# Long convolution and soft mixture of experts: the steps without the first stage rearranged, additions moved to GpSimd, the last batch's rows loaded in two parts, and a new order for the last pairs

## Chip, cores and metric

The kernel runs on one core of a Trainium2 chip. The metric is the device time of one execution in microseconds, as the median of several runs. All data are fp32.

## The reference, cut to what matters

```python
Xf = np.fft.rfft(x, n=2*S, axis=1)          # x: (8, 5696, 128), h: (5696, 128)
Hf = np.fft.rfft(h, n=2*S, axis=0)
y  = np.fft.irfft(Xf * Hf[None], n=2*S, axis=1)[:, :S, :]
x  = y.reshape(B*S, D)                       # 45568 tokens of 128
logits = x @ phi                             # 32 slots: 8 experts of 4
d = softmax(logits, axis=0)                  # over all tokens
slot_input = d.T @ x
slot_out[e] = relu(slot_input[e] @ w1[e]) @ w2[e]
c = softmax(logits, axis=1)                  # over the slots
return c @ slot_out
```

A causal convolution along the sequence by Fourier transforms comes first. Its result goes through a soft mixture of experts: a softmax over all tokens collects one input for each slot, small two-layer networks work on the slots, and a softmax over the slots hands the results back to the tokens. The first softmax needs the running maximum and sum over every token, so no output can be made before the last token has been seen.

## The kernel before, in words

The transform of length 2 x 5696 is factored into 90 by 64 by matrix products, and the work goes in stages that are pipelined over the steps of one loop (`for t in range(last_front + 1)`, L547). There are 9 images: the filter h and 8 batches.

Stage A (`stage_a`, L204) takes a chunk of an image, multiplies with a table (L211) and stores to the DRAM scratch `f`. It runs for t < NA = 72. Its input is folded on GpSimd (`fold`, L195).

Stage B works on units of which an image has 23, three to a step. `load_g` (L224) loads a unit of `f` on SP's queue, four units ahead. `stage_b1` (L235) is a group of small matmuls into the PSUM tile `bt` (L244), of which there is one buffer, and three VectorE operations: the products `pr` (L265) and `pi` (L268), which read PSUM, and their sum `yf` (L270), which reads two SBUF tiles. `stage_b2` (L274) takes `yf` through a second group of matmuls (L284), ScalarE copies the result (L288), and SP stores it to the DRAM scratch `z` (L289). b2 runs one unit behind b1.

Stage C works on pairs of column blocks, 4 to a batch, 32 in all, one to each two steps. `load_pair` (L309) loads a pair's rows of `z` in two transfers (block 0 of 64 rows, 1024 KB, and block 1 of 26 rows, 416 KB) into a tile `zc`. `stage_c1` (L323) has two halves of eight matmuls (L336); between the halves it calls the function `between`, and it returns a function `after`. The halves are folded on VectorE (L341, L342), and `after` does the second fold and four additions on GpSimd (L355), two of them on VectorE in the tail. `stage_c2` (L360) transposes the four quarters of y (L364); `stage_c3` makes logits (L373) and `lt`; `column_max` updates the running maximum on VectorE (L384 to L392); `stage_c4` (L398) transposes `lt` (L402), takes exponentials and row maxima, fills a part of `dt` on GpSimd (L410) and subtracts on GpSimd (L418); `stage_c5` transposes `dt` (L425); `softmax` (L431) normalises the rows, its last product on GpSimd (L438); `dispatch` (L442) accumulates the slot inputs (L449, L454); `stage_c6` (L469) transposes the combine weights (L473) and keeps them in the DRAM scratch `c_t`, or in the tail in the SBUF tile `cT`. In the tail `load_c` (L487) brings the kept weights back as tiles `cl`, four pairs at a time in two buffers, and `place_all` (L493) copies them into `cT` on GpSimd and ScalarE.

The schedule is manual: every engine runs its instructions in the order in which the program issues them, and each waits for its operands and its buffer. SP's queue has nearly all transfers, in that order too. `slot_b` (L561) puts in one b1 and the b2 of the unit before. In a step with odd t and t >= 72, before the change, the order is: slot, c1 of pair T with c4 of pair T-1 between its halves, slot, load of pair T+1, the fold and additions of `after`, c5, slot, softmax. In a step with even t it is: dispatch, slot, c2, c6, slot, c3, slot, column_max. `last_front` is 80; that step has only two units, and pair 26 in c2 and c3.

In these steps z has one buffer, `zc`. After the loop a second tile `zd` is made in memory that the front has left; 6 rows of zeros are copied into it by a transfer (L643), and then pair 28, the first of the last batch, is loaded (L646). Its matmuls read 96 rows only (`used`). The first-layer weights w1 are loaded in eight transfers of 512 KB, one a step from t = 73 (L631) and the last after the loop (L647). The tail loop (L680) takes V = 27 to 31: c2, dispatch of V-1, c6 of V-2, c3, column_max, placing of kept weights, c1 of a later pair with c4 between, c5, softmax; the second-layer weights w2 are loaded in V = 28 and 29 (L713). V = 31 ends with `join_quarters` (L499), which brings four partial maxima together, and its dispatch.

Then come the slot networks (L723 to L778) with one c6 between (L756), and the output: for each batch, row groups of 4, 4 and 3 are multiplied (L803), copied by ScalarE and VectorE (L812, L810) and stored (L814) through five buffers `o`.

Of the kernel before, what the change touches and what calls it, by code (L numbers as in the profile page):

```python
# [74 lines left out]
def kernel(  # L75
# [159 lines left out]
    def stage_b1(u):  # L235
        g, i = divmod(u, NU)
        n = min(2, NP - 2 * i)
        t_ = gs.pop(u)
        tag = "bz" if g == 0 and i % 2 else "bt"
        bt = bps.tile([P, 2, 512], F32, name="bt", tag=tag)  # L240
        for a in range(2):
            r = slice(a * HP, (a + 1) * HP)
            for q in range(n):
                nc.tensor.matmul(bt[q * HP:(q + 1) * HP, a, 0:2 * D], wt[r, 2 * i + q, :],  # L244
                                 t_[r, q, :, :].rearrange("p c d -> p (c d)"),
                                 start=True, stop=True)
        r = slice(0, n * HP)
        pv = bt[r, :, 0:2 * D].rearrange("p a (c d) -> p a c d", c=2)
        if g == 0:
            for a in range(2):  # L250
                pr = bpool.tile([P, 2, D], F32, name="ph", tag="pi" if a else "pr")
                for c in range(2):
                    nc.scalar.activation(pr[r, c, :], pv[:, a, c, :], AF.Copy,  # L253
                                         scale=turn[r, 0, i, a:a + 1])
                nc.vector.scalar_tensor_tensor(  # L255
                    out=Hr[r, i, a, :], in0=pv[:, a, 1, :], scalar=turn[r, 1, i, a:a + 1],
                    in1=pr[r, 0, :], op0=AL.mult, op1=AL.add)
                nc.vector.scalar_tensor_tensor(
                    out=Hi[r, i, a, 0, :], in0=pv[:, a, 0, :], scalar=turn[r, 1, i, a:a + 1],
                    in1=pr[r, 1, :], op0=AL.mult, op1=AL.subtract, reverse1=True)  # L260
            nc.gpsimd.tensor_scalar(out=Hi[r, i, :, 1, :], in0=Hi[r, i, :, 0, :], scalar1=-1.0,
                                    scalar2=None, op0=AL.mult)
            return
        pr, pi = [bpool.tile([P, 2, 2, D], F32, name=f"p{c}", tag=f"p{c}") for c in "ri"]
        nc.vector.tensor_tensor(out=pr[r, :, :, :], in0=pv,  # L265
                                in1=Hr[r, i, :, :].unsqueeze(2).broadcast_to([n * HP, 2, 2, D]),
                                op=AL.mult)
        nc.vector.tensor_tensor(out=pi[r, :, :, :], in0=pv, in1=Hi[r, i, :, :, :], op=AL.mult)  # L268
        y_ = bpool.tile([P, 2, 2, D], F32, name="yf", tag="yf", bufs=2)
        nc.vector.tensor_tensor(out=y_[r, :, :, :], in0=pr[r, :, :, :], in1=pi[r, :, ::-1, :],  # L270
                                op=AL.add)
        prods[u] = y_
# [23 lines left out]
    zn = used = None  # L296
# [12 lines left out]
    def load_pair(T):  # L309
# [3 lines left out]
        t_ = zring.pop(0)  # L313
        zring.append(t_)
        w_ = 2 * 2 * CH * 2 * D
        for r, n, p in z_blocks(N1):
            nc.sync.dma_start(
                out=t_[p:p + n, :, :, :, :, :].rearrange("k h o n c d -> k (h o n c d)"),
                in_=zd[b].rearrange("q (a r) c d -> (q a) (r c d)",
                                    a=2)[r:r + n, j * w_:(j + 1) * w_])  # L320
        zs[T] = t_

    def stage_c1(T, between):  # L323
        t_ = zs.pop(T)
        kr = used if t_ is zn else P
# [7 lines left out]
        def product(o, tab, q):  # L333
            p = bank()
            for h_ in range(2):
                nc.tensor.matmul(p[h_ * HP:(h_ + 1) * HP, :], i1[0:kr, tab, :],  # L336
                                 t_[0:kr, h_, o, :, q, :], start=True, stop=True)
# [9 lines left out]
        between()  # L347
        b_, a_ = product(1, 1, 0), product(1, 2, 1)
        nc.scalar.activation(om[:, :, :], b_, AF.Copy)

        def after():
# [6 lines left out]
        return after  # L358

    def stage_c2(T):  # L360
        for k in (3, 1, 0, 2) if tail else (3, 2, 1, 0):
# [185 lines left out]
    for t in range(last_front + 1):  # L547
# [22 lines left out]

        for tab, src, first, n, k in ((wt, t_w, LAG_B - 2, NP, 2 * PER),
# [5 lines left out]
        if t < NA:  # L577
            stage_a(t, 0)
            fold(t + 1, 0)
# [4 lines left out]
        if t == last_front:  # L584
            assert T is None and U is None and not us[1:]
            slot_b()
            stage_c2(pair(1))
            slot_b()
            assert not us and not wait_b2
            V = pair(1)  # L590
            stage_c6(V - 2)
            stage_c3(V)
            column_max(V)
            break
        rows = (lambda: None) if U is None else (lambda: stage_c4(U))
        after = None
        if T is not None:
            after = stage_c1(T, rows)
        else:
            rows()  # L600
        if pair(1) is not None:
            stage_c2(pair(1))
# [5 lines left out]
        if t < NA:  # L608
            load_x(t + 3)
# [4 lines left out]
        if t < NA:  # L614
            stage_a(t, 1)
            fold(t + 1, 1)
# [9 lines left out]
        if t == NA:  # L626
            lead.close()
            wts = inner.enter_context(tc.tile_pool(name="wts", bufs=1, side="right"))
            w1s = wts.tile([P, E, F], F32, name="w1s")
        if NA < t <= NA + E:  # L630
            nc.sync.dma_start(out=w1s[:, t - NA - 1, :], in_=moe_w1[t - NA - 1])  # L631

    T = V + 1
    (_, n0, p0), (_, n1, p1) = z_blocks(N1)
    gap, used = slice(p1 + n1, p0), p0 + n0
# [4 lines left out]
    zn = last.tile([P, 2, 2, CH, 2, D], F32, name="zd")  # L642
    nc.sync.dma_start(out=zn[gap, :, :, :, :, :].rearrange("k h o n c d -> k (h o n c d)"),  # L643
                      in_=zring[0][gap, :, :, :, :, :].rearrange("k h o n c d -> k (h o n c d)"))
    zring.insert(0, zn)
    load_pair(V + 2)  # L646
    nc.sync.dma_start(out=w1s[:, E - 1, :], in_=moe_w1[E - 1])  # L647
# [5 lines left out]

    after = stage_c1(T, lambda: stage_c4(V))
    after()
    stage_c5(V)
    softmax(V)
# [22 lines left out]
    for V in range(T, NT):  # L680
        if V > T:
            stage_c2(V)
        dispatch(V - 1)
        stage_c6(V - 2)
        if V == T:
            stage_c2(V)
# [6 lines left out]
        if N < NT:  # L693
            after = stage_c1(N, lambda: stage_c4(V))
            load_pair(N + 2)
        else:
            stage_c4(V)
        if after:
            after()
# [3 lines left out]
        if V == NT - 1:  # L703
            join_quarters()
            dispatch(V)
        softmax(V)
        if V == T:
            ybufs.insert(0, y_)
            stage_c1(T + 2, lambda: None)()
            load_pair(T + 4)  # L710
        else:
# [4 lines left out]
    stage_c6(NT - 2)  # L716
    assert list(Ls) == [NT - 1] and not (ys or ds or prods or gs or zs or xs or folded or wait_b2
# [26 lines left out]
    for g in range(EG):  # L744
        for f0 in range(0, F, FH):
            p = bank()
            for q in range(Q):
                nc.tensor.matmul(p[q * NSL:(q + 1) * NSL, :], siz[:, g * Q + q, :],
                                 w1s[:, g * Q + q, f0:f0 + FH], start=True, stop=True)
# [6 lines left out]
    stage_c6(NT - 1)  # L756
# [34 lines left out]
    assert NV * RW == R1 - 1  # L791
    G4 = 4
    for b in range(B):
        for w0 in range(0, NV, G4):
            n = min(G4, NV - w0)
            lone = b == B - 1 and w0 + G4 >= NV
# [53 lines left out]
```

## Time and profile before

| | us |
|---|---|
| median of 5 runs | 952.52 |
| lowest and highest of them | 948.92, 963.72 |
| the profiled execution | 950.38 |
| span of its profile | 948.6 |
| TensorE busy | 845.9 |
| VectorE busy | 670.4 |
| ScalarE busy | 522.6 |
| GpSimd busy | 446.4 |

The mean clock that TensorE was granted is 0.95 of full speed. The page of the profile has the busy time of each engine, then the span in 40 equal slices with the busy share of each in tenths and the granted clock (PEclk), then the transfers, then the chain of waits that ended last, and then groups of instructions, where PE is TensorE, DVE VectorE, ACT ScalarE, POOL GpSimd and SP SyncE. A line of a group gives the line of the code, the engine, the operation, output and inputs with their shapes, the count, the busy time in us and the mean in ns, and the idle time of the engine ahead of them with what ended it. L numbers are lines of the kernel before.

### The profile page before, as it was taken

To read this page: it belongs to the slowest core of one execution; us is meant where nothing else is said; L and a number is where in the kernel's file an instruction comes from. 1 tells how busy PE (TensorE), PEld (TensorE's weight loads), DVE (VectorE), ACT (ScalarE), POOL (GpSimd) and SP (SyncE) were. 2 spreads that over 40 slices of the span, in tenths; PEclk is the share of its full clock that TensorE was granted. 3 is DMA by queue.
4 is the path that set the end of the run, shared out by engine and by line. 5 is a ranking of instruction groups with operands and counts; after the bars stand their busy time and mean duration, and the time that the engine had idled before them with its cause. 6 is when DMAs were issued, how large, how long until landed. Compare 5 with 4: busy or idle time off the path is not lost.

```text
span 948.6 us, 20396 instructions
## 1 busy us (share of the span) xinstructions
PE 845.9 (89%) x7220; PEld 405.1 (43%) x7220; DVE 670.4 (71%) x1140; ACT 522.6 (55%) x1068; POOL 446.4 (47%) x408
## 2 busy tenths in 40 slices
PE   6867788889999999999999999989998887877893
PEld 2322233334444444444444444434443334345883
DVE  3034577577878878887888788868889996593552
ACT  3557645445666665665666566656664443385442
POOL 4646533235655555555555555545543333482000
PEclk9989999999999999999999999999999997797955
DMA  6998899999999999999999999999988976862698
GB/s 171 273 277 266 263 334 311 308 328 299 313 280 318 313 293 294 315 316 292 309 309 318 283 299 338 295 273 308 309 275 288 310 256 193 254 225 97 251 406 333
DMA packets 174239, 272.51 MB, mean 287 GB/s; under 512 B 14982, under 2 KB 119686, under 8 KB 171253
## 3 DMA queue, kind: packets, MB, share of 16 engines
q1 hardware_dynamic: 173563, 270.86, 89.9%
q8 instruction: 58, 0.95, 0.4%
q10 hardware_dynamic: 576, 0.36, 0.2%
q14 instruction: 42, 0.34, 0.1%
HBM read 142.85 MB, written 128.21 MB: 286 GB/s over the span
## 4 chain that ended last, share of the span: by engine, by line
PE 63%; DMA 21%; DVE 4%; issue 4%; POOL 3%; ACT 2%; SPq 2%; DVEq 0%; ACTq 0%; POOLq 0%
PE bank L211 20%; PE bank L336 12%; PE bt L244 10%; DMA gt<-f 7%; DMA f<-fst 7%; PE bz L284 7%; DMA out_dram<-o 4%; PE bank L364 3%; POOL y L355 2%; PE bank L449 2%; PE bank L402 2%; PE bank L373 2%; PE bank L425 2%; DMA zc<-z 1%; PE bank L473 1%
## 5 line engine op out<-in xcount | busy, mean ns | idle before, releaser
L211 PE MATMUL bank<-x,s 128*128 128x512 f32 x576 | 286.4, 625 | 9.8 <-POOL x L200 8.1
L200 POOL TENSOR_TENSOR x<-xc 128x512 f32<-128x512 f32 x144 | 183.5, 1276 | 145.4 <-PE bank L211 108.3
L213 ACT ACTIVATE fst<-bank 128x512 f32<-128x512 f32 x288 | 168.3, 597 | 93.8 <-PE bank L211 69.7
L288 ACT ACTIVATE zst<-bz 128x512 f32<-128x512 f32 (+1 forms) x184 | 108.3, 588 | 169.8 <-PE bz L284 156.4
L265 DVE TENSOR_TENSOR pr<-bt,Hr 128x512 f32<-128x512 f32 (+1 forms) x184 | 127.0, 690 | 103.0 <-PE bt L244 100.0
L244 PE MATMUL bt<-gt,wt 64*64 64x256 f32 x1620 | 138.0, 403 | 50.0 <-DMA gt<-f 17.2
L270 DVE TENSOR_TENSOR yf<-pr,pi 128x512 f32<-128x512 f32 (+1 forms) x184 | 153.7, 835 | 6.4
L211 PEld LDWEIGHTS bank<-x,s 128*128 128x128 f32 x576 | 100.5, 193 | 133.5 <-issue 88.9
L268 DVE TENSOR_TENSOR pi<-bt,Hi 128x512 f32<-128x512 f32 (+1 forms) x184 | 125.2, 681 | 0.0
L284 PE MATMUL bz<-yf,vt 64*64 64x256 f32 x1440 | 116.7, 383 | 6.0 <-DVE yf L270 3.9
L336 PE MATMUL bank<-zc,i 128*64 128x512 f32 x480 | 119.4, 621 | 0.0
L244 PEld LDWEIGHTS bt<-gt,wt 64*64 64x64 f32 x1620 | 44.4, 132 | 166.7 <-PE bank L211 58.8
L355 POOL TENSOR_TENSOR y<-y,op 128x512 f32<-128x512 f32 x64 | 77.6, 1212 | 71.5 <-DVE op L341 69.0
L355 POOL TENSOR_TENSOR y<-y,om 128x512 f32<-128x512 f32 x54 | 76.4, 1414 | 2.1
L410 POOL MEMSET dt<- 64x8 f32 x32 | 3.4, 107 | 146.4 <-ACT dn L413 80.8
L284 PEld LDWEIGHTS bz<-yf,vt 64*64 64x64 f32 x1440 | 53.7, 133 | 41.9 <-issue 11.6
L255 DVE SCALAR_TENSOR_TENSOR Hr<-bt,turn,ph 128x128 f32<-128x128 f32 (+1 forms) x46 | 16.0, 349 | 75.7 <-ACT ph L253 75.7
L364 PE MATMUL bank<-ident,y 109*128 109x109 f32 x512 | 58.8, 269 | 2.2 <-POOL y L355 1.5
L364 PEld LDWEIGHTS bank<-ident,y 109*128 109x128 f32 x512 | 51.2, 146 | 15.0 <-issue 11.6
L366 ACT ACTIVATE yt<-bank 128x360 f32<-128x360 f32 x128 | 51.8, 472 | 4.8 <-PE bank L364 4.8
L336 PEld LDWEIGHTS bank<-zc,i 128*64 128x64 f32 x480 | 30.0, 139 | 54.6 <-issue 48.4
L803 PE MATMUL op<-so,cT 32*128 32x128 f32 x704 | 46.3, 369 | 4.9 <-ACT o L812 4.4
(97 smaller groups left out, 893.7 us busy)
## 6 DMA issues: line engine op xcount, KB each, us to landing
f<-fst SPq DMA_DIRECT2D x288, 180.0 KB
gt<-f SPq DMA_DIRECT2D x198, 256.0 KB
z<-zst SPq DMA_DIRECT2D x176, 256.0 KB
zc<-z SPq DMA_DIRECT2D x30, 1024.0 KB
xc<-in_x_dram SPq DMA_DIRECT2D x64, 320.0 KB
out_dram<-o SPq DMA_DIRECT2D x16, 1024.0 KB
zc<-z SPq DMA_DIRECT2D x30, 416.0 KB
out_dram<-o SPq DMA_DIRECT2D x8, 768.0 KB
```

Of the source, the lines that this page charges most:

```text
L200: nc.gpsimd.tensor_tensor(out=y_[:, :, :], in0=t_[:, 0, :, :], in1=t_[:, 1, ::-1, :], op=AL.subtract if comp else AL.add)
L211: nc.tensor.matmul(p[:, :], s1[:, tab[G], :], src[:, :, :].rearrange("p n d -> p (n d)"), start=True, stop=True)
L213: nc.scalar.activation(st[:, :, G, :], p[:, :].rearrange("p (n d) -> p n d", d=D), AF.Copy)
L244: nc.tensor.matmul(bt[q * HP:(q + 1) * HP, a, 0:2 * D], wt[r, 2 * i + q, :], t_[r, q, :, :].rearrange("p c d -> p (c d)"), start=True, sto ...
L265: nc.vector.tensor_tensor(out=pr[r, :, :, :], in0=pv, in1=Hr[r, i, :, :].unsqueeze(2).broadcast_to([n * HP, 2, 2, D]), op=AL.mult)
L268: nc.vector.tensor_tensor(out=pi[r, :, :, :], in0=pv, in1=Hi[r, i, :, :, :], op=AL.mult)
L270: nc.vector.tensor_tensor(out=y_[r, :, :, :], in0=pr[r, :, :, :], in1=pi[r, :, ::-1, :], op=AL.add)
L284: nc.tensor.matmul(bz[a * HP:(a + 1) * HP, q, 0:2 * D], vt[r, i, a, :], y_[r, a, :, :].rearrange("p c d -> p (c d)"), start=True, stop=True)
L288: nc.scalar.activation(st[:, 0:n, :], bz[:, 0:n, 0:2 * D], AF.Copy)
L336: nc.tensor.matmul(p[h_ * HP:(h_ + 1) * HP, :], i1[0:kr, tab, :], t_[0:kr, h_, o, :, q, :], start=True, stop=True)
L355: eng.tensor_tensor(out=part_, in0=part(v, 0), in1=o_[:, :, :], op=sign)
L364: nc.tensor.transpose(p[:, i * TR:(i + 1) * TR], ys[T][0:TR, k * CH + i, 0:D], ident[0:TR, 0:TR])
```

## The change

It has these parts.

1. Steps with t >= 72 get a function of their own, `without_a`, and a slot of another form, `slot_around`, that puts b1 of a unit ahead of a part of stage C and b2 of the unit before behind it. `stage_c1` no longer takes `between`; it returns `second`, the second half, which returns `after`. `stage_c2` takes the quarters that it is to do.
2. `stage_b1` takes the engine of the addition `yf`. In these steps four of six go to GpSimd; in the last step (t = 80) the additions of both units stay on VectorE.
3. A second z buffer `zd` is made at t = 72 in the memory that stage A leaves, filled with zeros by GpSimd (128x4096), and put ahead of `zc` in the ring. The copy of zero rows and the 96-row matmuls are gone. The load of pair 28 is split: block 0 is issued at the head of the last step, block 1 after its last z store.
4. w1 becomes two tiles. The first four experts are loaded at t = 73 to 76; the other four in one transfer of 2 MB in the tail, after the load of pair 31.
5. The tail loop ends at V = 30 and takes c2 and c3 of pair 31 in beside c4 of pair 30. c4, c5 and dispatch of pair 31 follow the loop, then the last kept weights are placed. c6 of both last pairs stands between the two layers of the slot networks.
6. In the first batch the output's row groups are 1, 3, 4 and 3.

The diff, cut to its core:

```diff
-    def stage_b1(u):
+    def stage_b1(u, adder=nc.vector):
...
-        nc.vector.tensor_tensor(out=y_[r, :, :, :], in0=pr[r, :, :, :], in1=pi[r, :, ::-1, :],
-                                op=AL.add)
+        adder.tensor_tensor(out=y_[r, :, :, :], in0=pr[r, :, :, :], in1=pi[r, :, ::-1, :],
+                            op=AL.add)
...
-        between()
-        b_, a_ = product(1, 1, 0), product(1, 2, 1)
-        nc.scalar.activation(om[:, :, :], b_, AF.Copy)
+        def second():
+            b_, a_ = product(1, 1, 0), product(1, 2, 1)
+            nc.scalar.activation(om[:, :, :], b_, AF.Copy)
+            return lambda: after(a_)
...
+        def slot_around(part, adder):
+            fresh = bool(us)
+            if fresh:
+                u = us.pop(0)
+                prefetch(u + AHEAD)
+                stage_b1(u, adder)
+                wait_b2.append(u)
+            part()
+            if len(wait_b2) > fresh:
+                stage_b2(wait_b2.pop(0))
+
+        def without_a():
...
+            if T is not None:
+                slot_around(lambda: add(stage_c1, T), nc.gpsimd)
+                def middle():
+                    stage_c4(U)
+                    add(kept_[0])
+                slot_around(middle, nc.gpsimd)
+                load_pair(pair(-2))
+                kept_[1]()
+                slot_around(lambda: stage_c5(U), nc.vector)
+                softmax(U)
+                return
+            if t == last_front:
+                load_pair(V + 2, (0,))
+            slot_around(lambda: dispatch(pair(3)), nc.vector)
+            slot_around(lambda: stage_c2(V, (3, 2)), nc.vector if t == last_front else nc.gpsimd)
+            slot_around(lambda: stage_c2(V, (1, 0)), nc.gpsimd)
+            if t == last_front:
+                load_pair(V + 2, (1,))
+            stage_c6(pair(5))
+            stage_c3(V)
+            column_max(V)
+
+        if t == NA:
+            lead.close()
+            wts = inner.enter_context(tc.tile_pool(name="wts", bufs=1, side="right"))
+            zn = wts.tile([P, 2, 2, CH, 2, D], F32, name="zd")
+            nc.gpsimd.memset(zn[:, :, :, :, :, :], 0.0)
+            zring.insert(0, zn)
+            w1s = [wts.tile([P, E // 2, F], F32, name="w1a")]
+        if NA < t <= NA + E // 2:
+            nc.sync.dma_start(out=w1s[0][:, t - NA - 1, :], in_=moe_w1[t - NA - 1])
...
-    zn = last.tile([P, 2, 2, CH, 2, D], F32, name="zd")
-    nc.sync.dma_start(out=zn[gap, :, :, :, :, :].rearrange("k h o n c d -> k (h o n c d)"),
-                      in_=zring[0][gap, :, :, :, :, :].rearrange("k h o n c d -> k (h o n c d)"))
-    zring.insert(0, zn)
-    load_pair(V + 2)
-    nc.sync.dma_start(out=w1s[:, E - 1, :], in_=moe_w1[E - 1])
+    w1s.append(last.tile([P, E // 2, F], F32, name="w1b"))
...
-    for V in range(T, NT):
+    for V in range(T, NT - 1):
...
         else:
             stage_c4(V)
-        if after:
-            after()
+            stage_c2(V + 1)
+            stage_c3(V + 1)
...
-        if V == NT - 1:
-            join_quarters()
+        if N == NT:
+            column_max(V + 1)
             dispatch(V)
         softmax(V)
         if V == T:
...
             load_pair(T + 4)
+            nc.sync.dma_start(out=w1s[1][:, :, :],
+                              in_=moe_w1[E // 2:].rearrange("e d f -> d e f"))
...
-    stage_c6(NT - 2)
+    stage_c6(NT - 3)
+    stage_c4(NT - 1)
+    stage_c5(NT - 1)
+    join_quarters()
+    dispatch(NT - 1)
+    softmax(NT - 1)
+    while landed:
+        placed_c()
...
-    stage_c6(NT - 1)
+    for T in list(Ls):
+        stage_c6(T)
...
-        for w0 in range(0, NV, G4):
-            n = min(G4, NV - w0)
+        for w0, n in ((0, 1), (1, 3), (4, 4), (8, 3)) if b == 0 else ((0, 4), (4, 4), (8, 3)):
```

## The prediction on record

> **What bounds the kernel now.** I read the page's 40 slices first. A slice is 23.7 us; digits are busy tenths.
> ```profile
> PE   6867788889999999999999999989998887877893
> DVE  3034577577878878887888788868889996593552
> POOL 4646533235655555555555555545543333482000
> PEclk9989999999999999999999999999999997797955
> ```
> TensorE (PE) fills slices 11 to 29. From slice 30 (711 us) on it has gaps, VectorE (DVE) reads 9, and at slice 33 the clock falls. From 711 us the first stage is finished, and this is what the change touches. The windows view, one line per two steps, then the last step (t = 80) with what follows:
> ```profile
> 719.29:738.90 19.61, 16.49 (x184) 7.51 (x187) 18.29 (x31) 9.38 (x19) 7.17 (x7) 1.00 0.91 306
> 738.90:758.52 19.62, 16.49 (x185) 7.51 (x187) 18.37 (x32) 9.39 (x19) 7.32 (x7) 1.00 0.89 298
> 758.52:778.15 19.63, 16.49 (x184) 7.51 (x187) 18.37 (x32) 9.38 (x19) 7.33 (x7) 1.00 0.85 285
> 778.15:797.40 19.25, 14.83 (x132) 7.70 (x134) 12.06 (x21) 6.69 (x13) 7.20 (x6) 0.76 0.55 176
> ```
> Columns after the length: PE, weight loads, VectorE, ScalarE, GpSimd, PE clock, DMA share, GB/s. A double step takes 19.6 us and VectorE is busy 18.3 of it: VectorE bounds it, with TensorE waiting in turn. The chain of waits (start, us, what) of one double step agrees:
> ```profile
> 719.95 0.69 DVE pr L265
> ...
> 721.27 0.69 DVE yf L270
> 721.97 0.61 DVE op L341
> ...
> 722.65 1.20 POOL y L355
> ...
> 723.91 2.78 POOL y L355 x2
> ...
> 726.76 1.21 POOL y L355
> ...
> 728.01 0.59 PE bank L364 x4
> ```
> So c2 also waits for the last of four GpSimd additions. In the tail the same view shows transfers:
> ```profile
> 801.56 9.80 DMA zc<-z
> ...
> 811.55 3.30 PE bank L336 x8
> ...
> 820.09 8.95 DMA zd<-z
> ...
> 843.02 8.49 DMA cl<-c_t
> ```
> c1 of pair 28 starts 3.4 us late, and its eight matmuls take 3.30 us where the same eight take 1.87 at full clock: the wait costs twice.
>
> **What the Trainium skill says.** "TensorE: Matmul & The Clock Gate", What's actually happening: the clock halves after an idle window of about 3.4 us and needs as long a busy one to recover. The trace agrees: after gaps around 784 to 788 us the windows show 0.50 from 789 to 798, and again 813 to 822. "GPSIMD Engine Reference", Performance versus the Vector engine: a two-input fp32 addition is about 2 times slower than on VectorE. The groups by form:
> ```profile
> L270 DVE TENSOR_TENSOR yf<-pr,pi 128x512 f32<-128x512 f32 x18 | 15.0, 833 | 0.6
> L355 POOL TENSOR_TENSOR y<-y,om 128x512 f32<-128x512 f32 x6 | 8.5, 1415 | 0.2
> L355 POOL TENSOR_TENSOR y<-y,op 128x512 f32<-128x512 f32 x6 | 7.1, 1187 | 6.8 <-DVE op L341 6.6
> ```
> Here it is 1.19 us alone and 1.41 beside VectorE. "SBUF — State Buffer", Who interferes with whom: a VectorE operation with two SBUF inputs contends with GpSimd, one with a single SBUF input does not. The trace agrees: yf is 0.69 us alone and 1.11 beside GpSimd; pr and pi (one input in PSUM) stay at 0.68.
>
> **The change, part by part.** I walked the new program order of each engine by hand with the trace's spacings (VectorE: pr, pi 0.6 each, fold 0.7 each, yf 0.7 or 1.05; TensorE: b1 0.6, b2 0.45, c1 half 1.87, c4 and c5 0.6, dispatch 1.02, c2 half 0.83, c6 0.5, c3 0.75).
>
> *1. Double steps.* Four of six yf leave VectorE; the two that stay are those beside L355. 4 x 0.7 = 2.8 us go: 18.3 becomes 15.5. But two new idles come. The next b1 waits for the single bt buffer, and with yf gone nothing fills that gap on VectorE: 0.75. And column_max now follows c3 with no unit between. From the last b1 TensorE does half of c2, b2, c6 and c3 (2.53), ScalarE's lt 0.6 more: 3.15, of which pr and pi fill 1.3; 1.85 idle, with the next pr queued behind. 15.5 + 2.6 = **18.1 us** in place of 19.6. Other bounds are below: TensorE's spacings sum to about 15.0 to 16.5, GpSimd 7.2 + 4 x 1.19..1.41 = 12.0 to 12.8, DMA 306 GB/s x 19.6/18.1 = 331 GB/s (slices reach 338) in the two double steps with w1, lower later since half of w1 moves out. The moved addition in the even step sits behind the four L355 and L438; I get its end 0.4 us ahead of its b2, so no wait. c2 no longer waits on L355. From b1 of unit 184 (714.31) to b1 of unit 205 (783.45) are 69.1 us now; 3 x 18.1 + 9.05 = 63.4 then: **gain 5.7**. Bounds: 2 (each moved addition exposed by 0.5 us) to 10 (TensorE-bound at 16.5, idles filled).
>
> *2. The zero fill of the new z buffer* (128x4096, GpSimd, at t = 72). No such row; the page's fills of 64x8 in 0.108 and 128x128 in 0.205 us give 0.8 ns an element, 3.4 us; VectorE's 128x4096 took 3.47. It queues behind L438, which ends at 710.3, or until 711.4 behind the store of the freed buffers: done at 713.7 to 714.9. The addition of unit 183, moved to GpSimd, queues behind it; then b2(183) on TensorE, and behind that c6, c3 and b1(184). 1.2 + 0.4 + 1.3 on top gives b1(184) at about 717.2 where it is 714.31: **loss 2.9** (0 to 4.5; zero if the first unit's load lands later anyway). TensorE idles 712 to 715; half a chance of half clock for some 1.5 us: **loss 0.8**.
>
> *3. Last step and z in two goes.* t = 80 now runs from b1(205) to the end of c3 in 12.6 us (783.45 to 796.05), much of it at half clock. In my walk TensorE's longest gap is 1.45 us, the clock holds, and it takes 8.3: **gain 4.3**. The last z store leaves 7.6 us after b1(205), where it was 10.8. Block 0 (1 MB) goes at the head of the step into a buffer free since c1 of pair 26. Block 1 (416 KB) waits for the store to land (now 2.8 us from its data at 794.2 to the load's issue at 797.0; I take 2.2, the copy of the gap rows being gone): issue at +9.8. At the 200 to 380 GB/s of those windows it moves in 1.1 to 2.1 us; with some 2 us to land, as for the store, it is there by +13 to +14. c1(28) is ready for it at +19.3. So the 3.4 us wait goes, and what is late next is VectorE. From c3's end to the fold of pair 28's second half are 23.6 us now (796.05 to 819.65). Without the wait (3.4), and with c1 of 27 and 28 and c4 at full clock (3.01, 3.30, 1.11, 3.64 in place of 1.87, 1.87, 0.59, 1.87: 4.9, some of it hidden) my walk has 15.6: **gain 8.0** (2 to 9). The gap copy on SP and the partial rows fall away at no cost: 96x64 and 128x64 matmuls share the 592 ns minimum.
>
> *4. w1's second half* (2 MB, one transfer) is queued on SP behind pair 31's load and ahead of the third cl load. With that load 3.5 MB, some 9 to 10 us at 350 to 400 GB/s, done 3 us ahead of where ScalarE and GpSimd take cl; what is hidden here is hidden by V = 28's VectorE work. **0** (loss up to 3).
>
> *5. New final order.* c2 and c3 of pair 31 move beside c4 of pair 30. ScalarE still stands at the fifth cl copy (DMA, 851.5), so little moves: by my walk c4(31) comes 0.9 us earlier (861.2 for 862.05), c6(30) leaves the path ahead of L723 (0.5), and comes back between hid and hidT (0.5): **gain 0.9** (-1.5 to 4).
>
> *6. Output.* The first store waits now for 32 matmul passes (1.29) and two copies (1.29). With one row group 0.3 + 0.65: it starts 1.7 us earlier, but only 256 KB; the transfers are the bound after that: **gain 1.0** (0 to 1.7).
>
> Sum: 5.7 - 2.9 - 0.8 + 4.3 + 8.0 + 0 + 0.9 + 1.0 = 16.2. The profiled execution took 950.4 (span 948.6 and 1.8 around it): 934.2. The median of the runs is 2.1 above it: **936**.
>
> **The rivals.**
> A: *The transfers take the tail's gain.* For: pair 28's load took 12 us from its issue (799.3 to 811.4) with others behind it, far over what 1.44 MB need, and if the tracking of z is by whole tensor, block 0 is not early. Then block 1 lands at +21.8 where c1 is ready at +19.3: 2.5 us, and with it the half clock (3.7): 6.2, so 942. Against: 416 KB instead of 1.44 MB. Chance 0.2.
> B: *The front gains more.* The fill hides (3.7 back) and column_max's idle is filled by other VectorE work (1 us in 3.5 double steps): 936 - 7.2 = 929. Against: VectorE and TensorE keep program order. Chance 0.2.
> C: *Slower: GpSimd becomes the bound of the double step.* It has one place: the even step's addition behind L418, four L355 and L438. At 1.41 us it ends 0.4 us in time. From about 2.6 us a pass it decides: the chain 7.55 + 4 x 2.8 + 1.05 + 2.8 = 22.6, then b2, c6, c3, lt: a double step of 25 instead of 18.1, x 3.5 = 24: 960. Against it are the rows above: 1.41 at worst. Chance 0.05.
>
> **How the numbers follow.** Forecast 936 with chance 0.55 (its own 932 to 940), A 0.2, B 0.2, C 0.05. The range takes in A and B with some of their spread: 927 to 945. Some 0.5% (5 us) is what a measurement of this kernel tells from no change; A and the forecast are faster, C slower, a doubled A near the same: 0.92, 0.03, 0.05.
>
> **What would show it.** 1: windows of double steps at 18.1 us, VectorE near 15.5, GpSimd near 12.5, VectorE idle ahead of L384 (mx). 2: a GpSimd fill near 711 us and b1(184) at 717. 3: clock 1.00 through 780 to 825, no DMA wait ahead of c1 of pair 28. 5: ScalarE still waiting for cl. 6: first store 2.6 us less 1.7 after the first L803. I am wrong if the double step stays above 19, if half clock persists in the tail, or if c1(28) or c1(29) waits for z.

## The result, and the profile after

The changed kernel takes 947.41 us (median of 37 executions, 938.53 to 959.43); the kernel before takes 956.56 us over its 72 executions. The ratio is 0.9921 with a 95% interval of 0.9902 to 0.9940: faster by 0.8%, or 7.5 us, where 16.2 us were forecast. Ratios leave out executions more than 1.5% above the fastest of their kernel, which is why this one says less than the difference of the medians (9.1 us), and the second profile of the kernel before that is used below (961.99 us; the fastest took 946.82) is of that kind. The time lies outside the range on record (927 to 945). The profiled execution of the changed kernel took 946.73 us (span 944.9), that of the kernel before 950.38.

The page of the changed kernel, the span in 40 slices:

```profile
DVE  3034567577878887888888788888886778773542
POOL 5636632235655554555555555565556565563000
PEclk9979999999999999999999999999999899997966
```

Against the slices before, counted from 1: GpSimd is at 5 and 6 from slice 31 to 35, where it was at 3 and 4, and VectorE, which read 9 in slices 31 to 33, is at 6, 7 and 7. The clock's dip in slices 34 and 35 (7 and 7 before) is gone, there is a new one in slice 32 (8), and the dip at 37 and in the last two slices is still there.

A double step of the changed kernel, from one column_max to the next, in a window with the same columns as before:

```profile
739.49:758.93 19.44, 16.32 (x182) 7.43 (x184) 16.13 (x28) 9.50 (x19) 12.66 (x11) 1.00 0.83 266
```

It is 19.4 us long, as the next one is, 0.2 less than before; VectorE's busy time fell from 18.3 to 16.1, and GpSimd's rose to 12.7 as expected. So VectorE now idles 3.3 us of each.

The gain by stages, from two profiled executions of each kernel (the second pair belongs to the first experiment below). c1(23) means the first matmul of c1 of pair 23, b1(184) that of b1 of unit 184.

| stage | before | after | gain | forecast |
|---|---|---|---|---|
| issue of pair 23's load to c1(23) | 12.1, 12.1 | 17.6, 17.8 | -5.6 | -3.7 |
| c1(23) to c1(27) (double steps, last step) | 81.1, 79.6 | 78.4, 75.9 | +3.2 | +10.0 |
| c1(27) to c1(30) | 33.2, 38.0 | 27.7, 24.4 | +9.5 | +8.0 |
| c1(30) to the first output matmul | 53.6, 56.8 | 56.1, 56.2 | -1.0 | +0.9 |
| first output matmul to the end | 65.8, 65.9 | 64.8, 64.8 | +1.0 | +1.0 |
| sum | 245.7, 252.3 | 244.6, 239.2 | +7.1 | +16.2 |

The sum is near the 7.5 us of the ratio, but it is the mean of 1.1 us in the first pair of executions and 13.1 in the second. The stages show where the 9 us went: 6.8 in the double steps and the step after them, 1.9 in the fill's wait, 1.9 in the stretch with the new final order, with 1.5 more than forecast in the tail to set against them. Stages differ by some us between executions of one kernel (33.2 and 38.0), so single us here are not settled.

### The profile page after: what moved, and what is told of

Read it like the earlier page. It is cut to its first block, busy times and chain, and to the rows that moved or that the text cites. A ratio compares the mean times of both kernels' runs of the same rounds, so it can differ in the third digit from the quotient of the medians.

```text
span 944.9 us, 20432 instructions
## 1 busy us (share of the span) xinstructions
PE 838.5 (89%) x7220; PEld 399.3 (42%) x7220; DVE 661.5 (70%) x1127; ACT 522.5 (55%) x1070; POOL 469.6 (50%) x424
## 4 chain that ended last, share of the span: by engine, by line
PE 67%; DMA 16%; issue 5%; DVE 5%; ACT 2%; POOL 2%; SPq 2%; DVEq 0%; POOLq 0%; ACTq 0%
PE bank L211 22%; PE bt L244 11%; PE bank L336 10%; PE bz L284 8%; DMA gt<-f 5%; DMA out_dram<-o 4%; PE bank L366 4%; DMA f<-fst 3%; PE bank L451 3%; PE bank L375 2%; PE bank L427 2%; PE bank L404 2%; DMA cl<-c_t 1%; SPq L217 1%; PE bank L475 1%
## 5 line engine op out<-in xcount | busy, mean ns | idle before, releaser
L270 DVE TENSOR_TENSOR yf<-pr,pi 128x512 f32<-128x512 f32 (+1 forms) x169 | 145.3, 860 | 5.9
L244 PEld LDWEIGHTS bt<-gt,wt 64*64 64x64 f32 x1620 | 45.2, 133 | 170.5 <-PE bank L211 56.1
L336 PE MATMUL bank<-zc,i 128*64 128x512 f32 x448 | 109.2, 610 | 0.7 <-DMA zc<-z 0.7
L357 POOL TENSOR_TENSOR y<-y,op 128x512 f32<-128x512 f32 x64 | 78.7, 1230 | 60.0 <-DVE op L341 57.4
L357 POOL TENSOR_TENSOR y<-y,om 128x512 f32<-128x512 f32 x54 | 74.4, 1378 | 2.1
L255 DVE SCALAR_TENSOR_TENSOR Hr<-bt,turn,ph 128x128 f32<-128x128 f32 (+1 forms) x46 | 16.1, 349 | 75.8 <-ACT ph L253 75.8
L368 ACT ACTIVATE yt<-bank 128x360 f32<-128x360 f32 x128 | 51.5, 471 | 16.2 <-PE bank L366 16.2
L366 PE MATMUL bank<-ident,y 109*128 109x109 f32 x512 | 56.8, 263 | 1.0 <-DVE y L357 0.7
L366 PEld LDWEIGHTS bank<-ident,y 109*128 109x128 f32 x512 | 49.1, 142 | 14.9 <-issue 13.5
L386 DVE TENSOR_REDUCE mx<-lt 64x1 f32<-64x360 f32 x64 | 33.0, 516 | 29.5 <-ACT lt L378 29.1
L440 POOL TENSOR_TENSOR L<-L,rs 128x512 f32<-128x512 f32 x32 | 44.8, 1399 | 11.3 <-DVE rs L439 5.2
```

Source lines behind the costliest of these rows:

```text
L270: adder.tensor_tensor(out=y_[r, :, :, :], in0=pr[r, :, :, :], in1=pi[r, :, ::-1, :], op=AL.add)
L336: nc.tensor.matmul(p[h_ * HP:(h_ + 1) * HP, :], i1[:, tab, :], t_[:, h_, o, :, q, :], start=True, stop=True)
L357: eng.tensor_tensor(out=part_, in0=part(v, 0), in1=o_[:, :, :], op=sign)
L366: nc.tensor.transpose(p[:, i * TR:(i + 1) * TR], ys[T][0:TR, k * CH + i, 0:D], ident[0:TR, 0:TR])
```

## The experiments

Theory T1, from the two traces: *the double step is a loop of dependent work over several engines and not one engine's busy time; the zero fill delays the front by its place in GpSimd's queue; the second half of w1 and the early block 0 cost or give something in the tail; the new final order gives nothing.* The rivals are, by part: that the idle comes from the single product buffers, that the GpSimd additions give the time, that nothing is gained from where transfers are put. Ratios below are against the kernel before, run on the same chip. Line numbers in a view are those of the kernel that it shows; in the changed kernel c2 is L366 (L364 before), c3 L375 (L373) and its copy lt L378, column_max L386 (L384), c6 L475 (L473), GpSimd's four additions L357 (L355), and the placing of the kept weights L497 (L495).

### Both kernels again

> The kernel before, unedited, for a second profile. Theory 1 (the two profiles differ by chance ahead of 700 us and in the tail's waits): double steps at 19.6 us again, the load of pair 23 issued some us earlier or later than 702.8, and the stretch from it to the end, 245.8 us in the first profile, longer by 2 to 6 us, since the medians differ by more than the profiles. Rival (the first profile is typical): 245.8 within 1 us.

> The changed kernel, unedited, on the same chip as the next ones: ratio 0.992. Theory 1: double steps at 19.4 us again, b1 of unit 184 some 16.6 us after the load of pair 23 (the fill of the second z buffer), a DMA wait of 2 to 4 us ahead of c1 of pair 30; where the clock halves differs. The stretch from pair 23's load to the end 244.6 us, within 3. Rival (one unlucky execution): double steps near 18.1 and no such waits.

The kernel before took 961.99 us in one execution (span 960.2); the changed one has a ratio of 0.9943 [0.9912, 0.9973]. The fill's delay is there again (17.8 us from pair 23's load to c1(23)), and the double steps again take 19.4. In this execution the first double step had no half clock, which the first profile had (21.9 us from column_max to column_max). From pair 23's load to the end the two kernels took 252.3 and 239.2 us, 6.6 more and 5.4 less than in the first profiles and both outside what was expected, so one trace does not tell some 5 us of the whole.

### The fill later

```diff
         if t == NA:
...
-            nc.gpsimd.memset(zn[:, :, :, :, :, :], 0.0)
...
         if t >= NA:
             without_a()
+            if t == NA:
+                nc.gpsimd.memset(zn[:, :, :, :, :, :], 0.0)
```

> The changed kernel with the fill of the second z buffer issued at the end of step 72 instead of its head. Theory 1 (the fill holds the addition of unit 183 on GpSimd, and TensorE behind it): b1 of unit 184 comes 12 to 12.5 us after the load of pair 23 instead of 16.6, TensorE keeps full clock there, and the time falls by 4 to 7 us: ratio to before 0.985 to 0.988. Rival (the first unit's load sets b1(184) in any case): less than 1 us, ratio 0.992.

The front of the changed kernel, GpSimd's timeline and then the chain of waits:

```profile
709.22 3.52 POOL L621 MEMSET zd<- 128x4096 f32 x1 [1.45 <-DMA z<-zst]
```

```profile
714.00 0.65 PE bz L284 x4
714.65 0.92 PE bank L475 x4
715.57 1.36 PE bank L375 x8
716.93 1.06 PE bt L244 x8
```

The fill waits 1.45 us for a store to land (the view names one of z), runs 3.52 us, and the addition of unit 183 stands behind it in GpSimd's order. TensorE waits for that addition until 714.00, comes back at half clock (four matmuls of L475 take 0.92 us, and 0.52 later), and b1 of unit 184 starts at 716.93. Now the same view of GpSimd with the fill behind the step's work:

```profile
710.20 1.25 POOL L270 TENSOR_TENSOR yf<-pr,pi 64x512 f32<-64x512 f32 x1 [2.14 <-DVE pi L268]
711.40 3.51 POOL L634 MEMSET zd<- 128x4096 f32 x1
```

The addition goes first, and the fill lies in a stretch in which GpSimd has nothing else. The ratio is 0.9890 [0.9851, 0.9930] from six executions, beside 0.9943 for the changed kernel on the same chip; c1(23) starts 13.4 us after its load, 4.3 earlier than with the fill ahead. T1 holds here: in the six executions, here and below, with an addition behind the fill c1(23) comes 17.3 to 19.0 us after its load, and in the five of its variants without one 12.8 to 13.4. The ratios differ by 0.5% (some 5 us), which fits, though their intervals overlap; T1 had wanted a little more (0.985 to 0.988).

### All additions on VectorE

```diff
-                slot_around(lambda: add(stage_c1, T), nc.gpsimd)
+                slot_around(lambda: add(stage_c1, T), nc.vector)
...
-                slot_around(middle, nc.gpsimd)
+                slot_around(middle, nc.vector)
...
-            slot_around(lambda: stage_c2(V, (3, 2)), nc.vector if t == last_front else nc.gpsimd)
-            slot_around(lambda: stage_c2(V, (1, 0)), nc.gpsimd)
+            slot_around(lambda: stage_c2(V, (3, 2)), nc.vector)
+            slot_around(lambda: stage_c2(V, (1, 0)), nc.vector)
```

> The changed kernel with all additions yf back on VectorE, the order kept. Theory 1 (a double step is VectorE's path from the column maximum to the fifth unit's product, 15.3 us, and TensorE's from there to the next maximum, 4.1; two of the moved additions lie on that path): the double step becomes 20.6 us instead of 19.4, and the fill no longer holds an addition, so step 72 is 4 us shorter; in all 0 to 2 us slower than the changed kernel, ratio 0.992 to 0.994. Rival (the moved additions come back as contention and waits on GpSimd, so that moving them is worth nothing): the double step stays at 19.4 to 19.6 and the time falls by 4 us, ratio 0.988.

A double step of this kernel:

```profile
761.80:782.60 20.80, 16.25 (x182) 7.39 (x184) 18.99 (x31) 9.51 (x19) 7.25 (x7) 1.00 0.75 236
```

The new order alone makes the double step longer by 1.2 us (20.8 for 19.6). Yet the ratio is 0.9922 [0.9892, 0.9951], no worse than the changed kernel's (0.9943 on the same chip): with no addition on GpSimd nothing stands behind the fill, and c1(23) is 12.8 us after its load. As put in, the four moved additions give 1.4 us a double step, 3.5 times, 4.9 us, and cost 4.9 us behind the fill. That balance is a sum and not settled to the us: in this trace c1(23) to c1(27) takes 84.1 us for 75.9, since the last step too is longer (11.7 us for 9.4), in part at half clock.

### Only the odd step's additions on GpSimd

The last two of the four replacements above, without the first two.

> The changed kernel with the two moved additions of each even step back on VectorE, those of the odd steps still on GpSimd. Theory 1 (the even step's two lie where VectorE waits for TensorE anyway, so moving them gives nothing, and they are what makes step 72 wait for the fill): double step 19.3 to 19.6, c1 of pair 23 at 12.5 to 13.5 us after its load instead of 17.6, 4 to 5 us less: ratio 0.986 to 0.991. Rival (each moved addition is worth its 0.7 us): double step 20.8, which eats the gain: ratio 0.993.

```profile
760.60:780.00 19.40, 16.36 (x183) 7.46 (x184) 17.47 (x29) 9.52 (x20) 10.12 (x9) 1.00 0.83 270
```

The double step stays at 19.4 with VectorE busy for 17.5 of it, and c1(23) is 12.8 us after its load; the ratio is 0.9904 [0.9871, 0.9937]. So the two additions moved in the even step give nothing to the double step, and one of them stands behind the fill at t = 72. All 1.4 us come from the odd step's two.

### The kernel before with the odd step's additions on GpSimd

```diff
-    def stage_b1(u):
+    def stage_b1(u, adder=nc.vector):
...
-        slot_b()
+        moved = nc.gpsimd if t > NA and t % 2 else nc.vector
+        slot_b(moved)
...
-        slot_b()
+        slot_b(moved)
```

> The kernel before with the additions of the first two units of each odd step without the first stage on GpSimd, nothing else. Theory 1 (the old double step of 19.6 us is a loop over GpSimd's four additions of c1, c2's last quarter and TensorE, as its chain of waits shows, and the moved addition of the second unit stands ahead of the four): double step 19.4 to 20.2, ratio 0.998 to 1.004. Rival (VectorE, busy 18.3 of 19.6, bounds it, as the prediction read it): double step 18.2 to 18.6, 3.5 to 5 us less, ratio 0.995.

A double step, in windows, and the part of its chain of waits that the odd step ends with:

```profile
759.40:779.00 19.60, 16.39 (x184) 7.45 (x180) 17.59 (x31) 9.38 (x19) 9.79 (x9) 1.00 0.89 296
```

```profile
766.00 0.61 DVE pi L268
...
766.74 1.27 POOL yf L270
768.00 1.15 POOL y L355
...
772.07 1.20 POOL y L355
...
773.31 0.59 PE bank L364 x4
```

VectorE has 0.8 us less to do, and the double step is as long as before: ratio 1.0023 [0.9996, 1.0050]. So VectorE's busy share did not bound the kernel before. Its double step, as the chain of waits has it, was a loop that goes from VectorE's products through an addition yf to GpSimd's four additions L355, to c2's transposes, which wait for the last of them, and on in TensorE's order. In this loop the edit changes nothing: from the end of the products to the first L355 are 1.4 us here (the addition on GpSimd) and were 1.4 before (the addition and op on VectorE, 721.27 to 722.65). That the two are alike is chance. So the run shows that less work on VectorE is not enough; it does not show what a shorter loop would give.

Three numbers belong together: the old order with the odd step's additions moved is 19.6, the new order without moved additions 20.8, both together 19.4. The order alone loses, the odd step's additions alone give nothing.

### Two buffers for the products

```diff
-                pr = bpool.tile([P, 2, D], F32, name="ph", tag="pi" if a else "pr")
+                pr = bpool.tile([P, 2, D], F32, name="ph", tag="pi" if a else "pr",
+                                bufs=2)
...
-        pr, pi = [bpool.tile([P, 2, 2, D], F32, name=f"p{c}", tag=f"p{c}") for c in "ri"]
+        pr, pi = [bpool.tile([P, 2, 2, D], F32, name=f"p{c}", tag=f"p{c}",
+                             bufs=2) for c in "ri"]
...
-        y_ = bpool.tile([P, 2, 2, D], F32, name="yf", tag="yf", bufs=2)
+        y_ = pr
```

> The changed kernel with two buffers each for the products pr and pi; the sum is written over pr to make room. Theory 1 (the wait of VectorE for GpSimd's sum ahead of the fifth and sixth unit, 1.45 us a double step, lies beside TensorE's path to the next maximum and costs nothing; only the 0.16 us ahead of the second unit is on the path): double step 19.2 to 19.4 us, ratio 0.992 to 0.995 as the changed kernel. Rival (the single product buffer turned the moved additions into a wait and is what ate the gain): double step 18.0 to 18.5, 3 to 5 us less, ratio 0.987 to 0.990.

A wait that VectorE has in the changed kernel, in its timeline, made the buffers a suspect (the last column is the idle time ahead and what ended it):

```profile
771.30 1.45 DVE L270 TENSOR_TENSOR yf<-pr,pi 128x512 f32<-128x512 f32 x1
...
775.65 0.69 DVE L265 TENSOR_TENSOR pr<-bt,Hr 128x512 f32<-128x512 f32 x1 [1.45 <-POOL yf L270]
```

The product waits 1.45 us until GpSimd has read the old one. With a second buffer three double steps take 19.2, 19.8 and 19.2 us, where the rival wanted 18.0 to 18.5: the rival falls. That c3 is late anyway behind that wait is how the chain of waits reads. The ratio is 0.9911 [0.9884, 0.9938]. Two of the three:

```profile
740.90:760.70 19.80, 16.74 (x190) 7.85 (x192) 15.82 (x28) 9.50 (x19) 12.68 (x11) 1.00 0.94 311
760.70:779.90 19.20, 16.28 (x182) 7.44 (x184) 15.82 (x28) 9.50 (x19) 12.69 (x11) 1.00 0.83 270
```

### c6 behind c3

On top of the edit with the odd step's additions alone:

```diff
-            stage_c6(pair(5))
             stage_c3(V)
             column_max(V)
+            stage_c6(pair(5))
```

> The even-step additions back on VectorE (as in e7) and, in the steps without the first stage, c6 issued behind c3 and the column maximum instead of ahead of c3. Theory 1 (a double step is VectorE's path from the column maximum to the fifth unit's product and TensorE's from there over c2, b2, c6 and c3 to the next maximum; c6's 0.5 us lies on it for nothing): double step 18.8 to 19.0 us instead of 19.4, 1.5 to 2 us less than e7: ratio 0.986 to 0.990. Rival (an engine's busy time bounds the double step: VectorE at 16, TensorE at 16.3 or GpSimd; the place of c6 doesn't matter): 19.4, ratio 0.990.

The chain of waits of the changed kernel at the end of a double step:

```profile
774.30 0.66 PE bt L244 x8
774.96 0.90 PE bank L366 x8
...
776.45 0.52 PE bank L475 x4
776.98 0.79 PE bank L375 x8
...
777.85 0.49 ACT lt L378
...
778.36 0.52 DVE mx L386
```

From the last b1 of the step, half of c2, b2, c6 (L475), c3 (L375) and ScalarE's lt stand ahead of column_max, and behind that VectorE's products of the next step. c6 has nobody waiting for it so soon. With it behind c3 the double step is 18.9 us, 0.5 shorter than with the odd step's additions alone, the length of c6's four matmuls:

```profile
759.20:778.10 18.90, 16.18 (x184) 7.45 (x184) 17.48 (x30) 9.59 (x20) 10.12 (x9) 1.00 0.86 283
```

Ratio 0.9846 [0.9807, 0.9886], from six executions. T1's loop is confirmed at this place.

### Both of these together

The edit above with two product buffers.

> e8 with two buffers for each of the two products as well. Theory 1: the 0.16 us ahead of the second unit goes too: double step 18.6 to 18.9, ratio 0.985 to 0.990, the lowest of all. Rival: as e8's, 19.2 to 19.4, ratio 0.990.

```profile
749.70:768.40 18.70, 16.12 (x184) 7.47 (x184) 17.18 (x30) 9.60 (x20) 10.13 (x9) 1.00 0.86 281
```

The double step takes 18.7 us, c1(23) comes 12.8 us after its load. The ratio is 0.9798 [0.9746, 0.9850], the median 935.87 us, from six executions: faster than the kernel before, and the interval lies below that of the changed kernel (0.9902 to 0.9940). The rest of the change is as it was.

### w1's second half later

```diff
-            nc.sync.dma_start(out=w1s[1][:, :, :],
-                              in_=moe_w1[E // 2:].rearrange("e d f -> d e f"))
...
+            if V == T + 2:
+                nc.sync.dma_start(out=w1s[1][:, :, :],
+                                  in_=moe_w1[E // 2:].rearrange("e d f -> d e f"))
```

The new lines stand behind the loads of w2.

> The changed kernel with the 2 MB transfer of w1's second half issued after the last of w2 instead of after the load of pair 31. Theory 1 (2 MB ahead of the kept weights cl delay them and the load of pair 30): no DMA wait over 0.6 us ahead of c1 of pair 30, the 3 us that ScalarE waits for cl down to 1 or less, from c1(30) to the first output matmul 54 us or less where it is 56; 1 to 4 us less, ratio 0.990 to 0.993. Rival (those transfers are slow by themselves, as in the kernel before, where ScalarE waits 3 us too): waits of 0.6 to 3.5 and 3 us again, ratio 0.994.

ScalarE's wait for the kept weights, in the list of waits (total, count, longest):

```profile
ACT cT L497 <- DMA cl<-c_t: 2.8, 2, 1.5
```

Before it was 3.3 us, in the changed kernel 3.0. From c1(30) to the first output matmul are 57.2 us, where T1 wanted 54 or less: T1 falls here. The 2 MB transfer does not make the kept weights late. The ratio is 0.9934 [0.9908, 0.9959]. In this run c1(30) had no wait for its rows, but it had none in five other runs here in which the transfer stayed where it was, so that proves nothing of the move.

### The old final order

```diff
-    for V in range(T, NT - 1):
+    for V in range(T, NT):
...
-            stage_c2(V + 1)
-            stage_c3(V + 1)
-        if N == NT:
-            column_max(V + 1)
+        if V == NT - 1:
+            join_quarters()
             dispatch(V)
...
-    stage_c6(NT - 3)
-    stage_c4(NT - 1)
-    stage_c5(NT - 1)
-    join_quarters()
-    dispatch(NT - 1)
-    softmax(NT - 1)
-    while landed:
-        placed_c()
+    stage_c6(NT - 2)
```

> The changed kernel with the tail loop as before: pair 31 in a turn of its own, one c6 between the two layers. Theory 1 (the new order is worth 0 to 1 us, since ScalarE stands at the kept weights in both): from c1 of pair 31 to the first output matmul 44.5 to 46.5 us as with the new order (45.5 and 46.4; 44.4 and 44.8 before); ratio 0.992 to 0.996. Rival (the new order saves the pair's serial turn): 48 to 50 us, ratio 0.997 to 0.999.

From c1(31) to the first output matmul are 45.6 us; with the new order 45.5 and 46.4, in the kernel before 44.4 and 44.8. The ratio is 0.9924 [0.9888, 0.9960]. The new final order is worth nothing that can be seen. Since the old order has the 45.6 us too, the order is not what made this stretch some 1 us longer than in the kernel before; what did stays open.

### Pair 28 loaded in one go

```diff
-            if t == last_front:
-                load_pair(V + 2, (0,))
...
             if t == last_front:
-                load_pair(V + 2, (1,))
+                load_pair(V + 2)
```

> The changed kernel with both transfers of pair 28's load behind the last z store (the second buffer kept, the early first block given up). Theory 1 (1 MB more behind the store takes the load past the point at which c1 of pair 28 is ready): from c1 of pair 27 to c1 of pair 28 13 to 16 us instead of 10.9, with a DMA wait of 2 to 5 us ahead of it and half clock behind; 3 to 6 us more: ratio 0.996 to 1.000. Rival (it was the buffer and the earlier store, not the early block): 10.9 to 11.5 us, ratio 0.993.

The issue of the loads on SP's queue, and TensorE's c1 of pair 28 in this kernel:

```profile
797.35 2.51 SPq L319 DMA_DIRECT2D zd<-z  x2
```

```profile
808.65 1.94 PE L336 MATMUL bank<-zd,i 128*64 128x512 f32 x8
```

The whole 1.44 MB are loaded from 797.35 on, as late as in the kernel before (796.97), and c1(28) at 808.65 does not wait for them; c1(27) to c1(28) are 11.0 us, as in the changed kernel. Ratio 0.9937 [0.9907, 0.9968]. T1 falls: the early block 0 isn't needed. That it was the buffer and the earlier store, as the rival has it, is not shown by that. In the kernel before the same load, issued at 796.97, was waited for until 811.55, for 3.4 us (and in the second execution for 7.6 us). Other things near it differ: there the copy of the zero rows goes before it and 512 KB of w1 go right behind it, ahead of pair 29's load. Which of them made it land late was not tried and stays open.

## Why the prediction was half right

**Step 1, the double steps, failed, and with it the reading that it rests on.** The text on record says "VectorE bounds it" of the old double step, from 18.3 busy of 19.6 us, and goes on to subtract what leaves VectorE. The kernel before with two additions less on VectorE kept its 19.6 us, so that share was no bound: by the chain of waits the loop through L355, c2 and TensorE's order held it. The prediction had even shown that c2 waits for the last addition of L355, and then counted its going as nothing. "Perfetto Trace Analysis", Identifying the Most-Contended Engine, would have led the same way: it takes the engine of highest occupancy for the one to relieve first. Here that was VectorE with 94% in the double step, and 0.8 us less of it gave nothing; the measurement decides.

The sum "15.5 + 2.6 = 18.1" measured 16.1 + 3.3 = 19.4. Its first term is too small since the two additions that stay take 1.20 and 1.45 us, where the text has 1.05 and they took 1.12 and 1.11 before. The groups by form of two double steps:

```profile
L270 DVE TENSOR_TENSOR yf<-pr,pi 128x512 f32<-128x512 f32 x4 | 5.3, 1326 | 0.1
L440 POOL TENSOR_TENSOR L<-L,rs 128x512 f32<-128x512 f32 x2 | 3.0, 1500 | 0.0
```

So moving four additions took 2.2 us off VectorE and not 2.8. "SBUF — State Buffer", Who interferes with whom, names the kind of contention that the prediction used, a VectorE operation with two SBUF inputs beside GpSimd, and the trace agrees; its size here is 0.5 and 0.8 us an addition, where the text has 0.35. What sets the size is when the addition starts beside GpSimd (the first point of the last section), which the prediction did not follow. Its "1.41 beside VectorE" for L355 is a mean too: the two were 1.63 and 1.20, and the one during which VectorE's addition began took 1.18. The second term: the wait ahead of the next product, 0.75 in the text, is 1.45 and ends with GpSimd's reading of the products; ahead of column_max VectorE idles 1.42 (1.85 in the text), and 0.16 elsewhere; the rest, some 0.3, lies between instructions. What holds the step together is now the path VectorE to TensorE to lt to column_max and back, 15.3 us on VectorE from mx to the fifth unit's pi (758.93 to 774.2), 4.2 from there to the next mx (778.36). From b1(184) to b1(205) are 67.7 us without a half clock, for the 63.4 of the text and 69.1 before; the first double step at half clock (21.9) costs 2.5 more in one of the two executions.

**Step 2, the fill: mechanism right, size wrong.** "Loss 2.9" and "loss 0.8" became 5.6. The place in GpSimd's queue, the 3.5 us of the fill (3.4 in the text) and the chain behind it are as put. Two terms were too small. Counted from the load of pair 23, the fill starts at 8.9 us and ends at 12.4, where the text has a start at 7.5 to 8.6 and an end at 10.9 to 12.1: 1.0 more than its middle. And b2, c6 and c3 behind it ran at half clock, 2.9 us (0.65 + 0.92 + 1.36) for the 1.7 of the text, and the b1 after them too, 0.5 more; the text had half a chance of that, at 0.8.

**Step 3, the last step and the tail: size right, cause not.** The last step, b1(205) to the end of c3, takes 9.4 us, where 12.6 were before (11.1 in the second execution) and 8.3 forecast: 3.2 and 1.8 gained for 4.3. In the stretch that the text takes next, from there to the fold of pair 28's second half, 15.4 us were measured and 15.6 forecast, for 23.6 before. From c1(27) to c1(30) the gain is 9.5 (5.5 and 13.6 in the two pairs); the kernel before with its odd step's additions on GpSimd, whose tail is the old one, took 35.4 us there, between the 33.2 and 38.0 of the table. The wait for z ahead of c1(28) is gone and the clock stays up, as put. But the reason of the text, block 0 early and a small block 1, is not needed for it: the size came out right without its reason, which is luck.

A transfer is still in the tail's chain, of pair 30 in place of 28, and the third load of kept weights behind it:

```profile
812.29 9.84 DMA zd<-z
...
824.26 14.04 DMA cl<-c_t
```

c1(30) waited 3.5 us in that execution (and c1(29) 0.7), 0.6, 1.1, 2.2 and 2.0 in others with the new tail and none in the rest; why it differs stays open.

**Step 4, w1's second half at nothing, holds.** ScalarE's waits for the kept weights are 3.0 us in both executions, for 3.3 and 2.8 before, and moving the transfer changes nothing that can be seen.

**Step 5, the final order at 0.9, failed** within its bounds (-1.5 to 4): the stretch got longer by 1.0 us, and the old order put back gives the same length. The prediction itself said that ScalarE stands at the kept weights; it should have stopped there. Between c1(31) and the output all four executions ran at half clock for 10 to 21 us (the first of the changed kernel around 861 to 872, at 0.53), which does not set the two orders apart.

**Step 6, the output at 1.0, holds**: 65.8 and 65.9 us became 64.8, in both pairs.

None of the rivals came true as put. C, GpSimd as the bound, is off: it is busy 12.7 of 19.4 us. The nearest is one that was not there: the step is a loop, and thinning one engine leaves it.

## What to carry to other kernels

When one engine is busy for 94% of a period, a loop over several engines may still be what sets it; before subtracting work from the busy engine, walk the loop once around, from one operation to the same one a period later, through every engine, and see whether the piece to be removed lies on it. An operation moved to an engine with an in-order queue also waits for whatever stands there, above all for rare long ones such as a fill, and those should go behind the work of the step that someone waits for. Price what stays behind on the first engine by what it will then overlap: here each such addition ended 0.55 us after the GpSimd operation during which it started.

## What the hardware showed that was not expected

- A 128x512 addition with both inputs in SBUF took 0.69 us on VectorE with GpSimd idle. Where it started during an addition or product on GpSimd, it ended 0.55 us after the end of that one: 77 of 77 such additions yf in the changed kernel's trace. So its length, 1.20 and 1.45 us in the double step and 1.12 and 1.11 before, is what was left of GpSimd's operation, and 0.55. That operation kept its usual 1.18 us, and the next one on GpSimd was longer: L357 took 1.51 for 1.18, the product L440 1.50 for 1.05. Both engines lose.
- In one execution of the changed kernel TensorE's clock was 0.57 on average from 732 to 739.5 us, after four us in which it had been busy for 2.55; in another execution of the same program the same stretch, with 2.56 us busy, had 1.00. "TensorE: Matmul & The Clock Gate", What's actually happening, tells of an idle window of fixed length that runs freely and is not reset when the kernel starts. That its place differs from one execution to the next would fit this; but there was work in the stretch, and the clock still fell. A step's cost by a half clock is therefore no fixed number.
- A load of 1.44 MB that was issued at about the same time in two kernels was there within 11.3 us in one, and made TensorE wait until 14.6 us after its issue in the other, in both of its executions. Which of the transfers around it decides was not found out.
